# Local attention, channel mix and conv GLU on one core: mix in six chunks across batches, pooled queries and keys summed on VectorE or GpSimd, another order of steps

## The chip, the core and the metric

One core of a Trainium2 chip runs the whole program in one launch. TensorE (PE) does the matrix products into PSUM, VectorE (DVE) and ScalarE (ACT) work elementwise, GpSimd (POOL) does small elementwise work and issues the DMAs that add while they write, SyncE (SP) issues the plain DMAs. The metric is the device time of one launch in microseconds, the median over runs. In the profile times count from the start of the span.

## The reference

Three stages follow each other. `q`, `k` and `v` are 4 batches of 8 heads, 576 positions, 64 wide; everything is float32.

```python
q_d = q.reshape(B, H, Sd, 4, D).mean(axis=3)          # k_d, v_d alike: 576 -> 144 positions
out_up = np.repeat(sm_attn(q_d, k_d, v_d), 4, axis=2)
mask = np.abs(pos[:, None] - pos[None, :]) < 4         # a band of 7 positions
scores = np.where(mask, scale * (q @ k.T), -1e9)
x = out_up + softmax(scores) @ v                       # x: 4 x 576 x 512
x_prev = x moved by one position, zeros first
xk = mu_k * x + (1 - mu_k) * x_prev                    # xr alike with mu_r
v = np.maximum(xk @ w_k, 0) ** 2 @ w_v                 # 512 -> 1024 -> 512, the mix
x1 = sigmoid(xr @ w_r) * v
h = np.maximum(x1 @ w_in, 0)                           # 512 -> 1024
out = (h * sigmoid(conv3(h, conv_w))) @ w_out          # 1024 -> 512
```

## The kernel before

The channels lie on the 128 partitions, the tokens along the free dimension; `T` = 2304 tokens in all. To keep float32 accuracy on the fast matmul path every factor is cut into a high and a low part, and a product of 128 x 128 weights is three matmuls (high x high, low x high, high x low). `weight` brings one 512 KB tile of raw bits through `st_d` (a ring of three), rebuilds the float on ScalarE and VectorE into `st_f` or `st_ff`, and writes high and low parts (`wk`, `wv`, `wr`, `wi`, `wo`).

*Attention.* `group(b, gp)` is four heads of one batch: there are two groups a batch, eight in all. A group loads queries and keys (`kq`), overlapping windows of values (`vw`) and pooled values (`vd`), computes banded scores (L564) and pooled scores (L629), exponentials and their normalisation, transposes (L705, L756), the pooled output (L724) and the local output (L775), and adds the two into `xT`, a ring of two batches. For batch 0 the pooled keys and queries `kqd` are summed by VectorE (L527). For batches 1 to 3 the host hands in four planes `kqp`; `load_sum` loads the first plane by SyncE and adds the other three by GpSimd's DMAs, each of which waits for the one before it. `vd` is brought in the same way. From batch 1 on there is one buffer each for `kq`, `kqd`, `vw` and `vd`.

*Mix.* `mix_prep(b, nh)` makes the mixed input of half a batch, 288 tokens, in four 128-channel tiles: ScalarE scales `x_prev`, VectorE adds the scaled `x`, ScalarE writes the high part and VectorE the low part into `xk` (two buffers). The first half batch, `first_mix`, runs on plain float32 weights while these arrive. The other seven are `mix(b, nh)`: eight up groups of 12 matmuls (L933), each followed by relu, square and the cut into `k2`, and eight down groups of 12 (L982), whose results go to DRAM as `v_d`. Two PSUM buffers `mm` alternate.

*Output half.* Six chunks of 384 tokens: `gate` (L1254), `hidden` (L1295) with the convolution on VectorE, `outp` (L1375). Its tiles lie where the mix's tiles lay: the gate's input in `xk`, `x1` in `k2`, two buffers `v` for the mix's results. `w_r` and half of `w_in` (`wi0`) are cut early into the pool `mid`, which opens when the tiles of the pool `first` (batch 0's second buffers, `st_ff`) are free; the other half (`wi1`) and `v` lie in a pool that opens when the attention is done.

*Order.* Each piece of work is a `step` with an engine and the keys that it reads and writes. The list `ORDER` says in which order the steps are emitted, so also how each engine's queue stands, and `SECOND` which of two possible engines a step takes. Engines work their queues in order; between engines semaphores wait.

## Time and profile before

| | |
|---|---|
| runs (3) | 575.22, 577.9, 578.13 us; median 577.9 |
| profiled execution | 576.07 us, span 574.4 us |
| granted TensorE clock, mean | 0.986 |
| TensorE busy | 551.3 us, 96% |
| VectorE, ScalarE busy | 393.7 us, 306.0 us |
| moved by DMA | 73.34 MB |

Busy shares are means over stages that differ: in the first stretch weights arrive and the attention of batch 0 runs, then mix and attention share the engines, and from about 319 us on the output half runs. What ends a wait is named by the engine and line that released it. A matmul's own time in the profile is longer than its step to the next, since matmuls overlap; lengths of runs of matmuls are read from the chain of waits.

### The profile page before, as it was taken

The page shows a single profiled execution, that of the slowest core. Times are in us where ns is not written, and L with a number is a line of the kernel's source. Part 1 is how long each engine was busy: PE and PEld are TensorE (multiplying, and loading weights), DVE is VectorE, ACT ScalarE, POOL GpSimd, SP SyncE. Part 2 cuts the span into 40 slices and gives each one's busy share as a digit, 9 for nine tenths or more (in the row PEclk, how much of TensorE's full clock was granted, in tenths as well). Part 3 has the DMA queues.
Part 4 walks back from the last instruction along what each step waited for, and adds up shares of the span by engine and source line. Part 5 has one row for each costly group of instructions (what it writes and reads, how often), then busy time and mean ns, then how long its engine had stood idle before and what let it go on. Part 6 is the DMA issues. An engine that isn't in the chain of part 4 may idle for free.

```text
span 574.4 us, 13973 instructions
## 1 busy us (share of the span) xinstructions
PE 551.3 (96%) x5796; PEld 504.5 (88%) x5796; DVE 393.7 (69%) x807; ACT 306.0 (53%) x738; POOL 45.7 (8%) x150
## 2 busy tenths in 40 slices
PE   6898999959999999899999999999999999999996
PEld 3676689959999999899999999999998998998985
DVE  5897777727557745566747678887876677655680
ACT  4777776636455565435548557465445454353341
POOL 5011012112111111000000000000000000000000
PEclk9989999979999999999999999999999999999999
DMA  8578795969686776317323230122100401010011
GB/s 338 183 172 239 244 308 124 316 131 342 158 201 169 173 233 153 95 38 266 114 79 126 92 138 9 48 93 74 56 2 18 148 1 46 11 55 2 0 38 73
DMA packets 31008, 73.34 MB, mean 128 GB/s; under 512 B 3168, under 2 KB 13920, under 8 KB 29920
## 3 DMA queue, kind: packets, MB, share of 16 engines
q1 hardware_dynamic: 26624, 64.18, 32.2%
q0 software_dynamic: 4320, 8.26, 9.1%
q8 instruction: 45, 0.74, 0.5%
q14 instruction: 19, 0.16, 0.1%
HBM read 58.28 MB, written 14.16 MB: 126 GB/s over the span
## 4 chain that ended last, share of the span: by engine, by line
PE 81%; DMA 9%; ACT 4%; DVE 3%; issue 2%; SPq 0%; POOL 0%; ACTq 0%; POOLq 0%; DVEq 0%
PE a L1375 17%; PE mm L933 15%; PE mm L982 12%; PE a L1295 8%; PE mm L1295 7%; PE a L1254 4%; PE mm L1254 4%; DMA st_d<-in_moe_w_v 3%; DMA kqd<-in_kqp 3%; PE a L775 2%; PE a L564 2%; PE mm L900 1%; PE a L724 1%; DMA v_d<-tmp 1%; DMA vw<-in_vw 1%
## 5 line engine op out<-in xcount | busy, mean ns | idle before, releaser
L1375 PE MATMUL a<-wk,wv 128*128 128x512 f32 x432 | 101.2, 390 | 0.0
L933 PE MATMUL mm<-xk,wk 128*128 128x288 f32 x672 | 94.6, 298 | 1.8 <-ACT tmp L917 1.5
L982 PE MATMUL mm<-k,wv 128*128 128x288 f32 x672 | 95.4, 298 | 0.1
L1375 PEld LDWEIGHTS a<-wk,wv 128*128 128x128 f32 x432 | 80.9, 188 | 15.6
L933 PEld LDWEIGHTS mm<-xk,wk 128*128 128x128 f32 x672 | 90.2, 189 | 3.1 <-ACT tmp L917 1.8
L982 PEld LDWEIGHTS mm<-k,wv 128*128 128x128 f32 x672 | 90.0, 188 | 1.6 <-issue 1.0
L1295 PE MATMUL mm<-k,wi 128*128 128x386 f32 x288 | 54.0, 338 | 0.3 <-DVE k L1281 0.3
L1295 PE MATMUL a<-k,wi 128*128 128x386 f32 x288 | 53.6, 338 | 0.4 <-ACT h L1323 0.4
L1295 PEld LDWEIGHTS mm<-k,wi 128*128 128x128 f32 x288 | 50.8, 188 | 1.3 <-DVE k L1281 0.8
L1295 PEld LDWEIGHTS a<-k,wi 128*128 128x128 f32 x288 | 50.8, 188 | 1.3 <-ACT h L1323 0.7
L1350 ACT ACTIVATE tmp<-tmp 128x384 f32<-128x384 f32 x48 | 24.7, 524 | 45.0 <-DVE tmp L1344 45.0
L952 ACT ACTIVATE tmp<-mm 128x288 f32<-128x288 f32 x56 | 22.8, 411 | 33.1 <-PE mm L933 24.2
L1362 DVE TENSOR_TENSOR wv<-tmp,wv 128x384 fp32r<-128x384 f32 x48 | 26.2, 553 | 12.8 <-ACT wv L1360 12.6
L1353 DVE SCALAR_TENSOR_TENSOR tmp<-tmp,h 128x384 f32<-128x384 f32 x48 | 26.4, 556 | 12.1 <-ACT tmp L1350 10.7
L1360 ACT CAST wv<-tmp 128x384 fp32r<-128x384 f32 x48 | 24.2, 510 | 14.9 <-DVE tmp L1353 14.9
L1344 DVE SCALAR_TENSOR_TENSOR tmp<-h,cw_sb,tmp 128x384 f32<-128x384 f32 x48 | 29.7, 619 | 2.6
L1341 DVE SCALAR_TENSOR_TENSOR tmp<-h,cw_sb,tmp 128x384 f32<-128x384 f32 x48 | 29.7, 618 | 2.6 <-DVE tmp L1340 0.5
L970 DVE TENSOR_TENSOR k<-tmp,k 128x288 fp32r<-128x288 f32 x56 | 24.9, 456 | 8.5 <-ACT k L963 6.6
L917 ACT COPY tmp<-mm 128x288 f32<-128x288 f32 x32 | 12.3, 399 | 27.6 <-PE mm L982 18.1
L1340 DVE TENSOR_SCALAR tmp<-h,cw_sb 128x384 f32<-128x384 f32 x48 | 20.0, 417 | 9.7 <-ACT h L1323 4.4
L1254 PE MATMUL a<-xk,wr 128*128 128x386 f32 x144 | 26.2, 337 | 0.0
L1254 PE MATMUL mm<-xk,wr 128*128 128x386 f32 x144 | 26.1, 337 | 0.0
(160 smaller groups left out, 848.6 us busy)
## 6 DMA issues: line engine op xcount, KB each, us to landing
vw<-in_vw SPq DMA_DIRECT2D x7, 1152.0 KB, 8.9
kq<-in_kq SPq DMA_DIRECT2D x6, 1152.0 KB, 10.2
...
```

Source lines behind the costliest of these rows:

```text
L933: nc.tensor.matmul(pst[:, 0:NH], lhsT=wk_t[wt][:, kt, mt * P:(mt + 1) * P], rhs=xk[:, xs, kt, :], start=(kt == 0 and g == 0), stop=(kt == ...
L970: ("DVE",), (dve(NH),), lambda e, r=r, kh=kh, kl=kl: e.tensor_sub(kl, r, kh.bitcast(F32)),
L982: nc.tensor.matmul(pst[:, 0:NH], lhsT=wv_t[wt][:, kt, mt * P:(mt + 1) * P], rhs=xs, start=(kt == 0 and g == 0), stop=(kt == KF - 1 and g = ...
L1254: nc.tensor.matmul(pst[:, 0:CW], lhsT=late["wr"][wt][:, kt, mt * P:(mt + 1) * P], rhs=r_t[xs][:, kt, :], start=(kt == 0 and g == 0), stop= ...
L1295: nc.tensor.matmul(pst[:, 0:CW], lhsT=late["wi%d" % (mt * P // HF)][wt][:, kt, mt * P % HF:mt * P % HF + P], rhs=x1s[xs][:, kt, :], start= ...
L1341: nc.vector.scalar_tensor_tensor(out=cv, in0=tap(0), scalar=cw[:, 0, mt:mt + 1], in1=cv, op0=ALU.mult, op1=ALU.add)
L1344: nc.vector.scalar_tensor_tensor(out=cv, in0=tap(2), scalar=cw[:, 2, mt:mt + 1], in1=cv, op0=ALU.mult, op1=ALU.add)
L1350: step("ACT", act(CH), lambda: nc.scalar.activation(cv, cv, AF.Tanh, scale=0.5), (), [cvk])
L1353: lambda: nc.vector.scalar_tensor_tensor(out=gt, in0=cv, scalar=1.0, in1=tap(1), op0=ALU.add, op1=ALU.mult),
L1360: step("ACT", act(CH), lambda: nc.scalar.copy(gh, gf), ["wv_old", gk], [("gh", j)])
L1362: ("DVE",), (0.56,), lambda e: e.tensor_sub(gl, gf, gh.bitcast(F32)),
L1375: nc.tensor.matmul(pst, lhsT=xs[:, tt * P:(tt + 1) * P], rhs=wo[wt][:, kt, :], start=(kt == 0 and g == 0), stop=(kt == KF - 1 and g == 2),)
```

## The change

Six chunks of tokens replace the eight half batches: two of 288 and four of 432, which run across batch borders, so a chunk's input is put together from one or two batches' `xT`. `xk`, `k2` and `tmp` are 432 wide; there is one `xk` instead of two, and `xk` and `k2` lie in the pool `mid`, where `wi0` lay. All of `w_in` goes to the late pool. One of the two `v` buffers lies in `mid`, the other in the dead part of `k2`. `kqp` is gone: from batch 1 on each group's pooled keys and queries are summed from `kq`, by one reduction on VectorE or three additions on GpSimd, as `SECOND` says; nine of the twelve halves go to GpSimd. `ORDER` and `SECOND` are new lists; the warm-up matmuls stand at the front.

```diff
...
     NH = S // 2
+    NT = 3 * S // 4
+    chunks_ = [(0, NH), (NH, NH)] + [(t, NT) for t in range(S, B * S, NT)]
+    K2 = 9
...
-    xk_t = several(main, 2, [P, 2, KM, NH], F32R, "xk")
-    K2 = 9
-    k2_t = several(main, 2, [P, K2, NH], F32R, "k2")
-    tmp = main.tile([P, 8, NH], F32, name="tmp")
+    tmp = main.tile([P, 8, NT], F32, name="tmp")
...
-            if b:
-                d, dk = g["kqd"]
-                load_sum(
-                    d.rearrange("p r s -> p (r s)"), [kqp[b, gp, :, t] for t in range(FAC)], 4 * SD,
-                    [(dk, i, pr) for i in (0, half) for pr in range(2)], SL[0],
-                )
...
+                def f(eng, t=t, d=d):
+                    o = d[:, a // FAC:e // FAC]
+                    i = t[:, a:e].rearrange("p (s t) -> p s t", t=FAC)
+                    if eng is nc.vector:
+                        eng.reduce_sum(o, i, axis=AX.X)
+                    else:
+                        eng.tensor_tensor(out=o, in0=i[:, :, 0], in1=i[:, :, 1], op=ALU.add)
+                        for j in range(2, FAC):
+                            eng.tensor_tensor(out=o, in0=o, in1=i[:, :, j], op=ALU.add)
...
+                ws = [(dk, i0, pr)] + ([(dk, half, pr)] if whole else [])
+                if b:
+                    step(
+                        both, (0.15 + 1.05e-3 * (e - a), 3 * pool((e - a) // FAC)), f, [(k, i0)], ws,
+                        slack=SL[i0 > 0],
                     )
...
+    def mix_prep(i):
+        t0, n = chunks_[i]
+        prog.tag = "mp", i
+        parts = []
+        for b in range(t0 // S, (t0 + n - 1) // S + 1):
+            parts.append((b, max(t0 - b * S, 0), min(t0 + n - b * S, S)))
...
+            xs = [("xT", b % 2, kt, c) for b, a, e in parts for c in (0, half) if (c == 0 or e > NH)]
+
+            def scaled(t=t, kt=kt):
+                for b, a, e in parts:
+                    o = b * S + a - t0
+                    nc.scalar.activation(
+                        t[:, o:o + e - a], xT[b % 2][:, kt, a:e], AF.Copy, scale=mus[:, 2, kt:kt + 1])
+
...
+            def whole(t=t, f=f, kt=kt):
+                for b, a, e in parts:
+                    o = b * S + a - t0
+                    nc.vector.scalar_tensor_tensor(
+                        out=f[:, o:o + e - a], in0=xT[b % 2][:, kt, 1 + a:1 + e], scalar=mus[:, 0, kt:kt + 1],
+                        in1=t[:, o:o + e - a], op0=ALU.mult, op1=ALU.add)
+
...
+            step(
+                "ACT", act(n), lambda kt=kt, f=f: nc.scalar.copy(late["xk"][:, 0, kt, 0:n], f), [fk, "mid"],
+                [("xk", 0, kt)],
+            )
...
-                            pst[:, 0:NH], lhsT=wk_t[wt][:, kt, mt * P:(mt + 1) * P], rhs=xk[:, xs, kt, :],
+                            pst[:, 0:n], lhsT=wk_t[wt][:, kt, mt * P:(mt + 1) * P], rhs=late["xk"][:, xs, kt, 0:n],
...
     def open_mid():
         first.release()
         late["mid"] = mid = tc.alloc_tile_pool(name="mid", bufs=1, reuse_waits="tile")
+        late["xk"] = mid.tile([P, 2, KM, NT], F32R, name="xk")
+        late["k2"] = several(mid, 2, [P, K2, NT], F32R, "k2")
         late["wr"] = several(mid, 2, [P, KM, DM], F32R, "wr")
-        late["wi0"] = several(mid, 2, [P, KM, HF], F32R, "wi0")
-
-    seconds = [("kq", 2), ("kq", 3), ("st_f", 2), ("st_f", 3)] + [(x, 1) for x in ("kqd", "vw", "vd", "probs", "pd")]
+        late["v"] = several(mid, 1, [P, KM, CW], F32, "v")
+
+    seconds = [("st_f", 2), ("st_f", 3)] + [(x, 1) for x in ("kq", "kqd", "vw", "vd", "probs", "pd")]
     step("", 0.0, open_mid, (), [k for k in prog.writer if root(k, seconds)] + ["mid"])
     late["two"] = True
     by_columns(w_r, lambda: late["wr"][0], lambda: late["wr"][1], KM, range(KM), "wr", ["mid"])
-    by_columns(
-        w_in, lambda: late["wi0"][0], lambda: late["wi0"][1], KM, range(KF // 2), "wi", ["mid"],
-    )
-    mixes = [(b, nh) for b in range(B) for nh in range(2)]
-    for i, (b, nh) in enumerate(mixes):
-        xk_next = None
-        if nh == 0:
-            store_x(b)
-        if i:
-            mix(b, nh, *xk)
-        if nh == 0 and b + 1 < B:
-            gs = [group(b + 1, gp) for gp in range(NG)]
-            for g in gs:
-                g["loads"](0, NB)
-                attend([g], 0, NB)
-        if i + 1 < len(mixes):
-            xk = mix_prep(*mixes[i + 1])
+    store_x(0)
+
+    def attend_batch(b):
+        for g in [group(b, gp) for gp in range(NG)]:
+            g["loads"](0, NB)
+            attend([g], 0, NB)
+
+    attend_batch(1)
+    mix_prep(1)
+    for i in range(1, len(chunks_)):
+        mix(i)
+        if i == 1:
+            store_x(1)
+        elif i < B:
+            attend_batch(i)
+            store_x(i)
+        if i + 1 < len(chunks_):
+            mix_prep(i + 1)
...
-        late["wi1"] = several(wb, 2, [P, KM, HF], F32R, "wi1")
-        late["v"] = several(wb, 2, [P, KM, CW], F32, "v")
+        late["wi"] = several(wb, 2, [P, KM, DFF], F32R, "wi")
...
+    def v_t(i):
+        if i:
+            return cutout(late["k2"][0], KM * CW, KM * CW, F32).rearrange("p (k c) -> p k c", k=KM)
+        return late["v"][0]
...
```

Three places of the new order. The first is TensorE's queue around the pooled scores of batch 2, group 0 (`kqd` read, `mm` the mix's PSUM), before:

```order
L775 MATMUL a_181<-pt_139,vw_133 64x32 x36
L775 MATMUL a_182<-pt_139,vw_133 64x32 x36
L982 MATMUL mm_178<-k_123,wv_117 128x288
...
L629 MATMUL a_182<-kqd_131 32x144 x20
...
L564 MATMUL a_181<-kq_129 32x38 x40
L933 MATMUL mm_177<-xk_122,wk_115 128x288
```

and now:

```order
L769 MATMUL a_177<-pt_135,vw_129 64x32 x36
L769 MATMUL a_178<-pt_135,vw_129 64x32 x36
L935 MATMUL mm_174<-xk,wk_115 128x288
...
L623 MATMUL a_178<-kqd_127 32x144 x20
...
L558 MATMUL a_177<-kq_125 32x38 x72
L985 MATMUL mm_173<-k_1205,wv_117 128x288
```

Before, batch 1's last local outputs were followed by three down groups, then came the pooled scores; now they stand behind the last up group of mix chunk 1, one group after those outputs, and the down groups come after them.

The second is VectorE's queue from the last weight tile of the first chunk (`st_ff`) to the inputs of mix chunk 1 (`xk`), before:

```order
L394 SCALAR_TENSOR_TENSOR st_ff_150<-st_d_110,st_ff_150 128x512
L854 TENSOR_TENSOR xk_121<-tmp,xk_121 128x288
L844 SCALAR_TENSOR_TENSOR tmp<-xT_119,mus,tmp 128x288 x2
L854 TENSOR_TENSOR xk_121<-tmp,xk_121 128x288 x2
L580 TENSOR_REDUCE sums_145<-a_181 128x2x9
```

and now:

```order
L383 SCALAR_TENSOR_TENSOR st_ff_146<-st_d_110,st_ff_146 128x512
L421 CAST wv_117<-st_ff_146 128x4x128
L840 SCALAR_TENSOR_TENSOR tmp<-xT_119,mus,tmp 128x288
L512 TENSOR_REDUCE kqd_127<-kq_125 128x288
L421 CAST wv_117<-st_ff_145 128x4x128
L425 TENSOR_TENSOR wv_118<-st_f_113,wv_117 128x4x128
...
L425 TENSOR_TENSOR wv_118<-st_ff_145,wv_117 128x4x128
L784 TENSOR_TENSOR xT_120<-a_177,od_139 128x9x32 x2
L784 TENSOR_TENSOR xT_120<-a_178,od_139 128x9x32 x2
L854 TENSOR_TENSOR xk<-tmp,xk 128x288 x2
L840 SCALAR_TENSOR_TENSOR tmp<-xT_119,mus,tmp 128x288 x2
L854 TENSOR_TENSOR xk<-tmp,xk 128x288 x2
```

The weight cuts, one pooled sum and the attention output of batch 1, group 0 now stand between the last weight tile and the first write of `xk`.

The third is GpSimd's queue for batches 2 and 3, before (it begins in batch 2):

```order
L386 DMA kqd_131<-in_kqp 128x576 x2
L386 DMA vd_135<-in_vp 80x512 x3
L386 DMA kqd_131<-in_kqp 128x576 x3
```

and now (the last of the four `vd` DMAs and the two behind it are those of batch 3, group 0, whose pooled sums are the additions that follow):

```order
L375 DMA vd_131<-in_vp 80x512 x4
L1211 MEMSET v_1209 128x4
L375 DMA vd_131<-in_vp 80x512 x2
L514 TENSOR_TENSOR kqd_127<-kq_125 128x288
L516 TENSOR_TENSOR kqd_127<-kqd_127,kq_125 128x288 x2
```

The adding DMAs of the pooled keys are gone from the queue, and the additions stand behind the adding DMAs of the values.

## Rows read from the trace of the kernel before

**Rows 1.** The page: busy time, share of the span and instructions of each engine.

```profile
PE 551.3 (96%) x5796; PEld 504.5 (88%) x5796; DVE 393.7 (69%) x807; ACT 306.0 (53%) x738; POOL 45.7 (8%) x150
```

**Rows 2.** Windows: stretch and length, busy per engine (instructions), clock, DMA share, GB/s.

```profile
5.60:74.60 69.00, 63.37 (x1124) 45.66 (x1123) 59.45 (x135) 48.30 (x124) 9.85 (x30) 0.95 0.73 230
45.50:74.60 29.10, 26.33 (x446) 19.28 (x445) 22.63 (x48) 22.16 (x56) 4.32 (x5) 1.00 0.75 225
78.20:574.40 496.20, 482.72 (x4652) 455.05 (x4651) 331.48 (x667) 253.13 (x605) 31.39 (x102) 0.99 0.37 111
120.00:130.00 10.00, 5.77 (x153) 4.65 (x160) 1.60 (x4) 3.24 (x14) 1.72 (x3) 0.66 0.65 127
```

**Rows 3.** Timeline of PE behind its longest wait: start, length, instructions [idle before].

```profile
124.23 1.69 PE L629 MATMUL a<-kqd 64*32 64x144 f32 x40 [5.80 <-DMA kqd<-in_kqp]
...
126.53 1.15 PE L564 MATMUL a<-kq 64*32 64x38 f32 x80
127.61 2.36 PE L933 MATMUL mm<-xk,wk 128*128 128x288 f32 x12
```

**Rows 4.** Timeline of POOL: DMAs that add, two stretches.

```profile
111.59 0.86 POOL L386 DMA_DIRECT2D kqd<-in_kqp  x1 [7.07 <-DMA kqd<-in_kqp]
119.43 0.87 POOL L386 DMA_DIRECT2D kqd<-in_kqp  x1 [6.98 <-DMA kqd<-in_kqp]
...
188.82 0.81 POOL L386 DMA_DIRECT2D vd<-in_vp  x1 [3.02 <-DMA vd<-in_vp]
192.62 0.81 POOL L386 DMA_DIRECT2D vd<-in_vp  x1 [2.98 <-DMA vd<-in_vp]
```

**Rows 5.** Chain that ended last: start, length, what; full runs of matmuls.

```profile
267.71 12.69 PE mm L933 x96
...
293.18 12.85 PE mm L933 x96
...
384.26 2.72 PE a L1375 x12
```

**Rows 6.** Timeline of PE: the same forms without a wait before.

```profile
64.09 0.96 PE L629 MATMUL a<-kqd 64*32 64x144 f32 x40
...
70.16 0.91 PE L564 MATMUL a<-kq 64*32 64x38 f32 x80
...
80.42 1.83 PE L933 MATMUL mm<-xk,wk 128*128 128x288 f32 x12
```

**Rows 7.** Groups by form on DVE: count | busy us, mean ns | idle before.

```profile
L790 DVE TENSOR_TENSOR xT<-a,od 128x288 f32<-128x288 f32 x24 | 9.7, 451 | 14.6 <-PE a L775 9.6 <-issue 4.9
...
L527 DVE TENSOR_REDUCE kqd<-kq 128x224 f32<-128x896 f32 x2 | 2.1, 1080 | 4.7 <-DMA kq<-in_kq 4.7
...
L432 DVE CAST wi<-st_f 128x512 fp32r<-128x512 f32 x4 | 1.7, 420 | 0.0
```

**Rows 8.** Groups by form on POOL.

```profile
L345 POOL MEMSET probs<- 128x1152 f32 x1 | 1.1, 1057 | 0.0
```

**Rows 9.** DMA issues: count, KB each, median us to landing.

```profile
kq<-in_kq SPq DMA_DIRECT2D x6, 1152.0 KB, 10.2
...
vd<-in_vp SPq DMA_DIRECT2D x6, 160.0 KB, 3.6
```

**Rows 10.** Chain that ended last: a weight wait, and the start of the mix.

```profile
58.61 6.99 DMA st_d<-in_moe_w_v
...
78.20 1.59 PE mm L933 x12
...
98.65 4.32 DMA kqd<-in_kqp
```

**Rows 11.** Timeline of DVE: last weight tile of the first chunk, a pass of 684 columns.

```profile
73.88 0.69 DVE L394 SCALAR_TENSOR_TENSOR st_ff<-st_d,st_ff 128x512 uint32<-128x512 uint32 x1
...
77.50 0.87 DVE L580 TENSOR_REDUCE sums<-a 128x18 f32<-128x684 f32 x1
```

**Rows 12.** Windows, line L933 alone: up matmuls between 78.2 and 98.65 us.

```profile
78.20:98.65 20.45, 13.82 (x96) 12.65 (x95) 1.00 0.74 219
```

More of the change, by code (lines that the diff above doesn't have):

```diff
@@ L859, in first_mix @@
+                lambda kt=kt, f=f: nc.vector.tensor_sub(
+                    late["xk"][:, 1, kt, 0:n], f, late["xk"][:, 0, kt, 0:n].bitcast(F32)),
+                [fk, ("xk", 0, kt), "mid"], [("xk", 1, kt)],
+            )
+        return fs
     def first_mix(xs):
@@ L910, in first_mix, with out_of_mix, mix @@
                 weight(w_v, lambda: wv_t[0], lambda: wv_t[1], a, 4, mt * P, "wv", use=down)
-            prog.tag = "dn", 0, 0
+            prog.tag = "dn", 0
             out_of_mix(mt, pst, pk, 0)
-    def out_of_mix(mt, pst, pk, t0):
-        i = count["vs"] = count.get("vs", -1) + 1
-        vs, vk = tmp[:, 6 + i % 2], ("tmp", 6 + i % 2)
-        step("ACT", act(NH), lambda: nc.scalar.copy(vs, pst[:, 0:NH]), (), [pk, vk])
+    def out_of_mix(mt, pst, pk, i):
+        t0, n = chunks_[i]
+        j = count["vs"] = count.get("vs", -1) + 1
+        vs, vk = tmp[:, 6 + j % 2, 0:n], ("tmp", 6 + j % 2)
+        step("ACT", act(n), lambda: nc.scalar.copy(vs, pst[:, 0:n]), (), [pk, vk])
         step(
-            "SP", dma_us(NH), lambda: nc.sync.dma_start(out=v_d[mt, :, t0:t0 + NH], in_=vs),
+            "SP", dma_us(n), lambda: nc.sync.dma_start(out=v_d[mt, :, t0:t0 + n], in_=vs),
             [vk], [("v_d", t0, mt)],
         )
-    def mix(b, nh, xk, key):
-        c0 = nh * NH
-        k2 = {}
-        prog.tag = "up", b, nh
+    def mix(i):
+        t0, n = chunks_[i]
+        prog.tag = "up", i
+        at = {}
         for mt in range(KF):
@@ L959, in square, with high @@
                     e.tensor_tensor(out=r, in0=r, in1=r, op=ALU.mult)
-            def high(e, r=r, kh=kh):
+            def high(e, r=r, j=j):
+                kh = late["k2"][0][:, j, 0:n]
                 if e is nc.scalar:
@@ L1107, in tile_local_attention__then__channel_mix__then__conv_glu @@
     by_columns(
-        w_in, lambda: late["wi1"][0], lambda: late["wi1"][1], KM, range(KF // 2, KF), "wi", ["late"], HF,
+        w_in, lambda: late["wi"][0], lambda: late["wi"][1], KM, range(KF), "wi", ["late"],
     )
@@ L1157, in tile_local_attention__then__channel_mix__then__conv_glu @@
     step("", 0.0, lambda: None, (), [k for k in prog.writer if k[0] == "xT" and k[1] == 1] + ["xT1"])
-    for i in range(2):
-        step("", 0.0, lambda: None, (), [k for k in prog.writer if k[0] == ("xk", i)] + [("xk_old", i)])
+    step("", 0.0, lambda: None, (), keys_of("xk") + ["xk_old"])
     step("", 0.0, lambda: None, (), keys_of("k2") + ["k2_old"])
@@ L1194, in vpads @@
         def vpads():
-            v = late["v"][vi]
+            v = v_t(vi)
             if lo == 0:
@@ L1201, in load_chunk @@
         if lo == 0 or hi == T:
-            step("POOL", 0.15, vpads, ["late"], [("v", vi)])
-        t0s = [t for t in range(0, T, NH) if t < e and t + NH > a]
+            step("POOL", 0.15, vpads, [v_old[vi]], [("v", vi)])
+        t0s = [t for t, n in chunks_ if t < e and t + n > a]
         step(
@@ L1206, in load_chunk @@
             lambda: nc.sync.dma_start(
-                out=late["v"][vi][:, :, a - lo + 1:e - lo + 1], in_=v_d[:, :, a:e].rearrange("k p s -> p k s")),
-            ["late"] + [("v_d", t, mt) for t in t0s for mt in range(KM)], [("v", vi)],
+                out=v_t(vi)[:, :, a - lo + 1:e - lo + 1], in_=v_d[:, :, a:e].rearrange("k p s -> p k s")),
+            [v_old[vi]] + [("v_d", t, mt) for t in t0s for mt in range(KM)], [("v", vi)],
         )
```

134 lines of the change are left out of this document (54 added, 80 removed), and 184 rows, old and new, of tables (ORDER, SECOND).

## The prediction

> **What bounds the kernel now.** I read the page's busy shares first: TensorE is busy 551.3 of 574.4 us [rows 1], so the reader should look for what TensorE's time is made of and for the few places where it waits. The windows by stage come next. They show two regimes [rows 2]. Up to about 74.6 us VectorE leads (59.45 of 69.0 us busy, and 59.45 - 22.63 = 36.8 of the 39.9 us before 45.5); there TensorE is "busy" with long, thin work. From 78.2 us to the end TensorE is busy 482.7 of 496.2 us at a mean clock of 0.99: every matmul taken out there shortens the run, and so does every wait. The waits of TensorE in time order then name one large wait: at 118.4 us it stands 5.80 us before the pooled scores of batch 2 (L629), released by the DMA that adds up the pooled keys and queries [rows 3]. The POOL timeline says why that is late: each of the three adding DMAs waits for the one before it, and they follow each other at 7.84 us (111.59 to 119.43) there, against 3.80 us at 188.82 to 192.62 [rows 4].
>
> The sum is made against the profiled execution: span 574.4 us, 576.07 us as timed, so 1.7 us lie around the span. It is 0.3% below the median of the runs, 577.9 us. Half a per cent (575.0 to 580.8 us) is about what a measurement of this kernel can tell from no change.
>
> **Fewer matmuls in the mix.** Seven mix chunks of 288 tokens with 192 matmuls each (the first chunk is worked otherwise and stays) become one of 288 and four of 432: 1344 matmuls become 960. Columns stay the same, since 1152 x 288 = 768 x 432. A matmul of 288 columns takes 12.69 / 96 = 132.2 ns in a full run of them, one of 512 takes 2.72 / 12 = 226.7 [rows 5]; on the line between them 432 columns come to 192.9 ns. So 1152 x 132.2 - 768 x 192.9 = 152.3 - 148.2 = 4.1 us; by the slowest full run of 96 (12.85) it is 154.2 - 148.6 = 5.6. I take 4.1. This lies in the stretch where TensorE ends last, so all of it counts.
>
> *A rule against this size.* The rows have some 12 ns per matmul beside its columns (132.2 - 288/2.4). The Trainium skill (TensorE: Matmul & The Clock Gate, Back-to-back issue gap) gives 2.5 ns for a warm one; by it the 384 matmuls less would be worth 1.0 us. The rows disagree with it here, and the measurement decides.
>
> **The adding DMAs go.** All 24 transfers of the pooled queries and keys go, 18 of them adding ones. The wait of 5.80 us goes with them. Behind it TensorE ran slower for a while: 40 pooled scores took 1.69 us against 0.96, 80 scores 1.15 against 0.91, 12 mix matmuls 2.36 against 1.83 [rows 3, 6], 1.5 us together; the granted clock of that stretch was 0.66 [rows 2], part of it at 1.2 instead of 2.4 GHz, after the idle time. So 7.3 us go. What is late there next is the sum that replaces them, below.
>
> **The sums on GpSimd and VectorE.** Twelve pooled halves: nine go to GpSimd as three additions each of 288 columns, three to VectorE as one reduction. VectorE: 1.08 us for 896 columns [rows 7], so 1.39 for 1152. GpSimd shows no two-input addition. The nearest row is a memset of 1152 columns, 1.06 us [rows 8]; a quarter of it, 0.26, is the lower bound, all of it the upper. An addition moves three streams of 288 columns, 864, so I take 0.8 us: 2.4 us for a half, 4.8 for both. Now three walks to the place where TensorE needs them:
> - Batch 2, group 0 (the old wait): the queries and keys land 10.2 us after issue [rows 9], then 4.8 us of sums, 15.0. TensorE has in between seven groups of 12 at 1.59 and attention pieces of 5.7 (from their lengths between 78.2 and 98.65): 16.8 us. No wait.
> - Batch 2, group 1: VectorE does one half and stands for the load; behind it in its queue are the normalisation and the last half of the next chunk's inputs. 10.2 + 0.4 of issue, 1.4, two passes of 0.87 and a small one (2.0), three 432-wide steps (0.6 each, between 0.45 and 0.69) and a ScalarE copy of 0.5: 16.3 us. TensorE has eight groups at 1.59 and 2.9 us of attention: 15.6. It waits 0.7 us.
> - Batch 3, group 0: both halves stand on GpSimd's queue behind three adding DMAs for the values. Landing of the first load 3.6 us [rows 9], two spacings of 3.8, 0.8 for issuing the third, 4.8 of sums: 16.8 us. TensorE has five groups of 2.33 and some 5.3 of attention: 16.9. Just in time.
>
> I book 1.0 us, with the hops between engines. What is queued behind a late sum on GpSimd are only the next values' DMAs.
>
> **The order at the start of the mix.** Before, mix chunk 1 starts at 78.2 us, 3.6 us after VectorE finished the last weight tile of the first chunk (73.88 + 0.69) [rows 10, 11]. Now its input tile lies where the first tiles lay, so it can be written only after the last of these is free, and the attention of batch 1, group 0 is put ahead of it. VectorE's order says how much it must do. Up to the last weight tile: four passes over 684 columns (0.87 each), three casts (0.42) and small ones of 0.6 more, six 288-wide steps (0.45 each) less: 3.5 + 1.3 + 0.6 - 2.7 = 2.7 us more [rows 7, 11]. VectorE idles 29.1 - 22.6 = 6.5 us in the second half of that stretch, for weights on their way. With less traffic a part may go, anything from none to all; I take 0.8, near the low end, since nothing else of the loads' order is lighter. So the last tile is done at 74.6 + 2.7 - 0.8 = 76.5. After it: two casts 0.84, the reduction 1.39, three 512-wide steps of 0.69 2.1, twelve 288-wide ones 5.4, a ScalarE copy 0.4: 10.1. Mix chunk 1 starts at 86.7, 8.5 us later. But by then TensorE has done what it did before between 78.2 and 98.65 beside its 96 mix matmuls: 20.45 - 12.7 = 7.7 us [rows 5, 10, 12]. Net 0.8 us lost. In those 10.1 us TensorE has only 5.4 us to do, so it idles about as long as in [rows 3]; I book the same 1.5 us of lower clock. Bounds: with all idle gone 4.9 us gained; with one more weight wait like the one of 6.99 us [rows 10], 8 us lost.
>
> **What costs nothing.** One input tile instead of two: its next writing waits for the last up matmul, and a down half of 8 x 1.59 or 8 x 2.33 us lies over it (the ScalarE copy that waits has the next exponentials behind it, the 1.0 us above holds them). All of w_in loaded after the attention: two chunks of 192 x 0.194 = 37 us hide eight tiles; uncovered, a tile would cost its landing, about 5 us. The output half keeps its matmuls. The warm-up matmuls put in front lie before the first scores, where VectorE leads.
>
> **Sum:** -4.1 - 7.3 + 1.0 + 0.8 + 1.5 = -8.1: span 566.3, 568.0 us as timed.
>
> **Rivals.**
> 1. *The start gets shorter.* VectorE's 6.5 us of idle for weights vanish with the traffic. For it: the DMA queues stand at 0.75 there [rows 2]. Against: the weights' loads still queue behind the large loads on SyncE. 568.0 - 5.7 = 562.3 us.
> 2. *GpSimd's additions hold VectorE up.* Nine of the 27 additions fall before mix chunk 1, where VectorE leads: if VectorE stands still in them, 9 x 0.8 = 7.2 us go on the path: 575.2 us, no change. The rows of before have no such pair side by side. (The Trainium skill, GPSIMD Engine Reference, Key points, says the two share SBUF interfaces when VectorE reads two inputs from SBUF; no run here shows it yet.)
> 3. *The wait comes back on GpSimd's queue, slower than before.* Batch 3, group 0: if the value DMAs follow at the 7.84 us of [rows 4] and not at 3.8, the chain is 3 x 7.84 + 5.6 = 29.1 us against 16.9: TensorE stands 12.2 us and then runs 1.5 us of lower clock: 568.0 + 13.7 = 581.7. It decides from a spacing of 6.6 us on, where 3s + 5.6 - 16.9 + 1.5 eats the 9.9 us against the median; from 7.5 us on it is slower by over half a per cent. For it: that is what happened to batch 2. Against: those spacings fell with 288 KB adding transfers, which are gone.
>
> **How the numbers follow.** Forecast 0.56, rival 1 0.19, rival 2 0.13, rival 3 0.12. The forecast's own range is 563 to 574 (the bounds of the start, 0.26 to 1.06 us per addition, 4.1 to 5.6 us for the matmuls). 559 to 580 leaves out rival 3 and little else. Faster than 575.0: 0.93 of the forecast, all of rival 1, a third of rival 2: 0.75. Slower than 580.8: rival 3 but for its lower edge, and a little of 2: 0.11. Same: 0.14.
>
> **What would show it.** In the profile after: no wait for pooled keys over 2 us anywhere; 96 matmuls of 432 columns in 18.5 us; the first mix matmul with the new tile near 86.7 us, after some 5 us of idle TensorE; GpSimd additions of about 0.8 us; the output half as long as before. Wrong it would be by a start after 92 us, by a TensorE wait at batch 3's pooled scores, or by additions above 1.1 us.

## The result and the profile after

The changed kernel takes 568.27 us (median of 4 runs, 566.07 to 568.48) beside 577.34 us of the kernel before (also 4 runs): ratio 0.984, 95% interval 0.9803 to 0.9877. 568.0 was predicted. The total was met, by terms of which several were off and cancel.

The page of the profiled execution (568.25 us, span 566.5), its row of busy times, answers to [rows 1]:

```profile
PE 547.7 (97%) x5412; PEld 496.8 (88%) x5412; DVE 397.6 (70%) x758; ACT 307.2 (54%) x715; POOL 57.6 (10%) x159
```

The windows by stage after the change, columns as in [rows 2] (stretch and length, busy time of TensorE, its weight loads, VectorE, ScalarE and GpSimd, clock, DMA share, GB/s): the last weight tiles of the first chunk, the way to mix chunk 1, the mix with the rest of the attention, the output half.

```profile
45.50:76.60 31.10, 29.52 (x450) 23.09 (x450) 28.62 (x54) 23.11 (x56) 3.24 (x4) 1.00 0.81 265
76.60:86.60 10.00, 7.39 (x282) 5.78 (x280) 9.91 (x18) 6.47 (x15) 5.71 (x7) 0.92 0.42 99
86.61:308.70 222.09, 221.28 (x2672) 206.91 (x2673) 143.06 (x262) 124.80 (x294) 29.12 (x38) 0.99 0.46 148
308.70:566.50 257.80, 252.29 (x1296) 233.94 (x1295) 179.92 (x341) 124.56 (x277) 5.13 (x64) 1.00 0.15 53
```

The kernel before, profiled anew (run before_again, span 574.1), the two stages that answer to the last two rows:

```profile
77.85:318.51 240.66, 233.12 (x3360) 223.49 (x3358) 153.16 (x329) 131.67 (x332) 24.98 (x40) 0.99 0.60 177
318.51:574.10 255.59, 250.24 (x1297) 232.00 (x1295) 179.13 (x340) 121.78 (x273) 5.60 (x62) 1.00 0.14 49
```

Read them as a sum: mix chunk 1 starts 8.8 us later, the mix is 18.6 us shorter, the output half 2.2 us longer, together 7.6 us. In the mix TensorE stands 222.09 - 221.28 = 0.8 us where it stood 240.66 - 233.12 = 7.5. In the second row VectorE is busy 9.91 of 10.0 us: it sets the start of the mix, and has nothing to wait for there.

The timeline of TensorE at the start of the mix, and at the place of the old wait [rows 3]:

```profile
83.53 0.96 PE L623 MATMUL a<-kqd 64*32 64x144 f32 x40 [1.73 <-DVE xT L784]
...
84.85 1.11 PE L558 MATMUL a<-kq 64*32 64x38 f32 x80
86.61 3.25 PE L935 MATMUL mm<-xk,wk 128*128 128x288 f32 x12 [0.65 <-ACT tmp L919]
...
90.65 3.92 PE L935 MATMUL mm<-xk,wk 128*128 128x288 f32 x24
...
109.12 0.96 PE L623 MATMUL a<-kqd 64*32 64x144 f32 x40
```

The first matmul with the new tile comes at 86.61 us. The last row shows the pooled scores of batch 2, group 0: no wait, 0.96 us for 40 as in [rows 6]. But behind the waits of 1.73 and 0.65 us the matmuls at the start run at the lower clock, 1.2 GHz (granted 0.50 from 86 to 90 us, 0.56 from 90 to 92): 12 in 3.25 us.

The chain that ended last, full runs of matmuls (as [rows 5]):

```profile
233.62 18.73 PE mm L935 x96
...
369.36 2.13 PE mm L1309 x12
```

96 matmuls of 432 columns take 18.73 us (18.79 the slowest), 195.1 ns each.

The timeline of GpSimd for batch 3, group 0 (as [rows 4]): the second and third of the adding DMAs for the values, then the pooled sums; behind it TensorE's pooled scores.

```profile
159.31 0.80 POOL L375 DMA_DIRECT2D vd<-in_vp  x1 [2.77 <-DMA vd<-in_vp]
162.95 0.80 POOL L375 DMA_DIRECT2D vd<-in_vp  x1 [2.84 <-DMA vd<-in_vp]
163.50 1.00 POOL L514 TENSOR_TENSOR kqd<-kq 128x288 f32<-128x288 f32 x1
...
167.99 2.29 POOL L516 TENSOR_TENSOR kqd<-kqd,kq 128x288 f32<-128x288 f32 x2
```

```profile
170.34 0.93 PE L623 MATMUL a<-kqd 64*32 64x144 f32 x32 [0.29 <-POOL kqd L516]
```

The DMAs follow at 3.6 to 3.7 us, the two sums take 6.8 us and end at 170.3; TensorE's pooled scores wait 0.29 us for them, the longest wait for pooled sums in the mix.

The timeline of VectorE beside GpSimd's additions, then the same two instructions in the run sums_vector (below), where GpSimd adds nothing:

```profile
77.39 1.35 DVE L512 TENSOR_REDUCE kqd<-kq 128x288 f32<-128x1152 f32 x1
...
78.98 1.43 DVE L425 TENSOR_TENSOR wv<-st_f,wv 128x512 fp32r<-128x512 f32 x1
80.34 1.20 DVE L840 SCALAR_TENSOR_TENSOR tmp<-xT,mus,tmp 128x288 f32<-128x288 f32 x1
```

```profile
79.91 0.68 DVE L422 TENSOR_TENSOR wv<-st_f,wv 128x512 fp32r<-128x512 f32 x1
80.51 0.51 DVE L837 SCALAR_TENSOR_TENSOR tmp<-xT,mus,tmp 128x288 f32<-128x288 f32 x1
```

GpSimd adds from 77.58 to 81.2 us. The two instructions with two inputs in SBUF inside that time take 1.43 and 1.20 us; without the additions they take 0.68 and 0.51. The reduction, with one input, keeps its 1.35.

### The profile page after: what moved, and what is told of

It reads as the page before. It is cut to its first block, busy times and chain, and to the rows that moved or that the text cites. A ratio compares the mean times of both kernels' runs of the same rounds, so it can differ in the third digit from the quotient of the medians.

```text
span 566.5 us, 13091 instructions
## 1 busy us (share of the span) xinstructions
PE 547.7 (97%) x5412; PEld 496.8 (88%) x5412; DVE 397.6 (70%) x758; ACT 307.2 (54%) x715; POOL 57.6 (10%) x159
## 3 DMA queue, kind: packets, MB, share of 16 engines
q0 software_dynamic: 1728, 2.95, 3.2%
## 4 chain that ended last, share of the span: by engine, by line
PE 78%; DVE 12%; DMA 3%; ACT 3%; issue 2%; POOL 1%; ACTq 0%; DVEq 0%; POOLq 0%; SPq 0%
PE a L1389 17%; PE mm L935 15%; PE mm L985 14%; PE mm L1309 8%; PE a L1309 8%; PE a L1268 5%; PE mm L1268 4%; DMA st_d<-in_moe_w_v 2%; PE a L769 2%; PE a L558 1%; PE a L750 1%; PE a L718 1%; PE a L699 1%; DVE st_f L380 1%; DVE st_f L383 1%
## 5 line engine op out<-in xcount | busy, mean ns | idle before, releaser
L935 PE MATMUL mm<-xk,wk 128*128 128x432 f32 (+1 forms) x480 | 94.5, 353 | 0.7 <-ACT tmp L919 0.7
L985 PE MATMUL mm<-k,wv 128*128 128x432 f32 (+1 forms) x480 | 91.1, 347 | 0.0
L935 PEld LDWEIGHTS mm<-xk,wk 128*128 128x128 f32 x480 | 86.0, 193 | 4.5 <-ACT tmp L919 1.0
L985 PEld LDWEIGHTS mm<-k,wv 128*128 128x128 f32 x480 | 84.2, 188 | 3.6 <-issue 0.4
L954 ACT ACTIVATE tmp<-mm 128x432 f32<-128x432 f32 (+1 forms) x40 | 20.2, 508 | 25.4 <-PE mm L935 20.8
L380 DVE SCALAR_TENSOR_TENSOR st_f<-st_f,st_d 128x512 uint32<-128x512 uint32 x28 | 21.1, 752 | 18.2 <-ACT st_d L399 18.2
L974 DVE TENSOR_TENSOR k<-tmp,k 128x432 fp32r<-128x432 f32 (+1 forms) x40 | 22.8, 579 | 12.3 <-ACT k L966 11.6
```

The costliest lines, as they stand in the source:

```text
L380: nc.vector.scalar_tensor_tensor(out=f, in0=f, scalar=3, in1=low, op0=ALU.logical_shift_left, op1=ALU.bitwise_or)
L935: nc.tensor.matmul(pst[:, 0:n], lhsT=wk_t[wt][:, kt, mt * P:(mt + 1) * P], rhs=late["xk"][:, xs, kt, 0:n], start=(kt == 0 and g == 0), sto ...
L985: nc.tensor.matmul(pst[:, 0:n], lhsT=wv_t[wt][:, kt, mt * P:(mt + 1) * P], rhs=late["k2"][xs][:, at[kt], 0:n], start=(kt == 0 and g == 0), ...
```

## The experiments

**Both kernels again.** No edit. The question is a difference that the change doesn't explain: 12 matmuls of 386 columns in the output half follow in 2.13 us, before in 2.10.

> The kernel before, unchanged, for a profile on the chip of the runs beside it. In the profiled runs so far 12 matmuls of 386 columns follow in 2.10 us before the change and in 2.13 after it, which is 1.3 us over the 48 x 12 of L1295 / L1309 alone, and nothing of them was changed. Theory: the length belongs to the chip or the execution; then before and after agree here to 0.01 us per 12. Rival: it belongs to the program (where tiles lie, what runs beside); then 2.10 and 2.13 come again, and the output half is again 255.7 us before and 257.8 after.

> The changed kernel, unchanged. Time 566 to 569 us, ratio 0.980 to 0.988. Theory (chip or execution): full runs of 96 matmuls of 432 columns as long as twelve times eight would be on the line through this chip's own 288 and 512 columns, and the output half as long as that of the kernel before on this chip to 0.5 us. Rival (program): 18.75 us for 96 and an output half 2.1 us longer than before.

Measured: 575.83 us for the profiled run of before (one run), 569.08 after, ratio 0.9867 (0.9841 to 0.9893) to 17 runs of before on that chip. There before has 2.10 to 2.11 again, after 2.13, and 18.73 us for 96 of 432 columns. The length belongs to the program, not to the chip.

**All pooled sums on VectorE.**

```diff
-    3, 7, 22, ..., 266, 278, 279, 290, 314, 325, ..., 472, 496, 497, 508, 532, ..., 618, 642, 643, 677, 689, ...
+    3, 7, 22, ..., 266, 290, 325, ..., 472, 508, ..., 618, 689, ...
```

> The changed kernel with all pooled sums on VectorE, none on GpSimd. Theory: GpSimd's additions stretch VectorE's two-input instructions that run beside them (0.68 to 1.43 us, 0.51 to 1.20 us; 4.3 us of excess before mix chunk 1), so VectorE is no worse off with three reductions of 1.35 us more (4.05 us): first mix matmul with the new tile at 86.6 +- 1.0 us, time within 1.5 us of the changed kernel. Rival: the additions cost VectorE nothing on its path; then the first such matmul comes 4 us later, at 90.6, and the time is 571 to 573 us.

Measured: 569.3 us, ratio 0.9876 (0.9848 to 0.9903), the same as the changed kernel beside it. Start of the mix:

```profile
86.10 3.25 PE L932 MATMUL mm<-xk,wk 128*128 128x288 f32 x12 [0.69 <-ACT tmp L916]
```

86.10 us, and not 90.6, with 4.05 us more of reductions on VectorE ahead of it. GpSimd takes no load off VectorE here: what it takes over ahead of the mix, VectorE loses to longer instructions.

**One part of the change in the kernel before.** For the last five groups additions on GpSimd stand where two of the three adding DMAs were issued.

```diff
-                load_sum(
-                    d.rearrange("p r s -> p (r s)"), [kqp[b, gp, :, t] for t in range(FAC)], 4 * SD,
...
+                    def add(prs, t=t, d=d):
+                        for pr in prs:
+                            o = d[:, pr, 0:2 * SD]
+                            i = t[:, pr, 0:2 * S].rearrange("p (s t) -> p s t", t=FAC)
+                            nc.gpsimd.tensor_tensor(out=o, in0=i[:, :, 0], in1=i[:, :, 1], op=ALU.add)
+                            for j in range(2, FAC):
+                                nc.gpsimd.tensor_tensor(out=o, in0=o, in1=i[:, :, j], op=ALU.add)
...
+                step("SP", 0.0, lambda: None, (), ks)
+                step("GQ", 0.0, lambda: None, (), ks)
+                step("GQ", 2.4, lambda: add(() if late_ else (0,)), () if late_ else [(k, 0)], ks)
+                step("GQ", 2.4, lambda: add((0, 1) if late_ else (1,)), [(k, 0)], ks)
```

> The kernel before with one part of the change alone: for the last five groups the adding DMAs of the pooled queries and keys are replaced by additions on GpSimd at the places in its queue where the last two adding DMAs of each group were issued; chunks, tiles and the rest of the order stay. Theory: the 5.8 us wait and the 1.5 us of slower clock behind it are the adding DMAs' price, so 7.3 us go: 570 us, ratio 0.987, no wait of TensorE for pooled keys over 1 us. Rival: the wait is only handed on, to the additions or to the value DMAs behind them: 575 us or more, ratio above 0.995.

Measured: 574.77 us, ratio 0.9974 (0.9951 to 0.9997). The theory fails on the time: of 7.3 us some 1.5 were gained. VectorE's timeline, while GpSimd adds from 83.9 to 91.0 us, then TensorE's:

```profile
85.04 1.18 DVE L436 TENSOR_TENSOR wv<-st_ff,wv 128x512 fp32r<-128x512 f32 x1 [0.96 <-ACT wv L430]
86.15 1.44 DVE L391 SCALAR_TENSOR_TENSOR st_f<-st_f,st_d 128x512 uint32<-128x512 uint32 x1
87.62 1.47 DVE L394 SCALAR_TENSOR_TENSOR st_f<-st_d,st_f 128x512 uint32<-128x512 uint32 x1
89.01 1.23 DVE L976 TENSOR_TENSOR tmp<-tmp 128x288 f32<-128x288 f32 x1
90.16 1.20 DVE L987 TENSOR_TENSOR k<-tmp,k 128x288 fp32r<-128x288 f32 x1
```

```profile
94.00 6.13 PE L950 MATMUL mm<-xk,wk 128*128 128x288 f32 x24 [1.42 <-ACT tmp L969]
...
116.95 6.56 PE L999 MATMUL mm<-k,wv 128*128 128x288 f32 x36
123.44 0.96 PE L646 MATMUL a<-kqd 64*32 64x144 f32 x40
...
143.00 1.86 PE L999 MATMUL mm<-k,wv 128*128 128x288 f32 x12 [1.71 <-ACT tmp L969]
```

Five instructions that take 0.69, 0.68, 0.69, 0.46 and 0.46 us in before_again take 3.5 us more in all. VectorE is late with the mix's `k`, ScalarE with the relu that empties the PSUM buffer, TensorE waits 1.42 us and then needs 6.13 us for 24 matmuls (3.44 in before_again), at a granted clock of 0.50. At 116.95 another 36 take 6.56 us instead of 5.03, again at 0.50, though TensorE had stood no longer than 0.24 us just before; why the clock fell there is open. So it comes to the pooled scores at 123.44, when the sums are ready, and only 0.9 us before the 124.37 of before_again. With the full clock behind it TensorE is 3.0 us ahead at 127.4 (before_again 130.35), and loses that again beside the next group's additions (136.8 to 143.2): it waits 0.68, 1.71 and 0.83 us where before_again waits 0.35, and at the pooled scores of group 1 it is 0.2 us behind (160.29 against 160.11). The lost time was not gone; it had moved beside the additions.

**The same with one input on GpSimd.** The kernel leaves out the sums: each of the three passes scales one position of four.

```diff
-                            nc.gpsimd.tensor_tensor(out=o, in0=i[:, :, 0], in1=i[:, :, 1], op=ALU.add)
-                            for j in range(2, FAC):
-                                nc.gpsimd.tensor_tensor(out=o, in0=o, in1=i[:, :, j], op=ALU.add)
+                            for j in range(1, FAC):
+                                nc.gpsimd.tensor_scalar(o, i[:, :, j], float(FAC), 0.0, op0=ALU.mult, op1=ALU.add)
```

> As before_sums, but GpSimd's three passes of each half read one input instead of two (scale of one position of four; the sum itself is left out). Theory: what ate the 7.3 us in before_sums are VectorE's two-input instructions that ran beside GpSimd's two-input additions (0.46 to 1.23 us, 0.69 to 1.47 us between 85.0 and 91.3 us) and held TensorE up behind them; with one input they keep their 0.46 and 0.69 us, TensorE has no wait over 1 us there, and the time is 569 to 571.5 us. Rival: VectorE is stretched beside any GpSimd pass, or the gain was lost elsewhere: 574 to 576 us.

Measured: 571.43 us, ratio 0.9929 (0.9903 to 0.9955), between before_sums and the changed kernel. VectorE and TensorE at the same places:

```profile
86.61 1.18 DVE L391 SCALAR_TENSOR_TENSOR st_f<-st_f,st_d 128x512 uint32<-128x512 uint32 x1
87.83 0.70 DVE L394 SCALAR_TENSOR_TENSOR st_f<-st_d,st_f 128x512 uint32<-128x512 uint32 x1
88.44 0.97 DVE L975 TENSOR_TENSOR tmp<-tmp 128x288 f32<-128x288 f32 x1
89.38 0.91 DVE L986 TENSOR_TENSOR k<-tmp,k 128x288 fp32r<-128x288 f32 x1
```

```profile
93.49 3.44 PE L949 MATMUL mm<-xk,wk 128*128 128x288 f32 x24 [0.26 <-ACT tmp L968]
...
119.20 0.96 PE L645 MATMUL a<-kqd 64*32 64x144 f32 x40
```

With one input VectorE is stretched less (1.18 instead of 1.44, 0.97 instead of 1.23; the 0.70 instead of 1.47 falls mostly between GpSimd's two halves, 87.3 to 88.2 us), the wait ahead shrinks to 0.26 us, the full clock stays, and TensorE is at the pooled scores 4.2 us sooner. The theory holds in its direction and falls in its detail: GpSimd's passes hold VectorE up with one input too, only less. The Trainium skill (SBUF — State Buffer, SBUF: two separate sides) says that VectorE and GpSimd share one pair of ports, that an instruction holds it to its end, and that VectorE wants it where it has two inputs in SBUF, against a GpSimd instruction that reads SBUF. The rows agree: about twice the length for those, none more for the reduction.

**The adding DMAs put back into the changed kernel.**

```diff
+                    def plane(eng, d=g["kqd"][0]):
+                        nc.sync.dma_start(out=d.rearrange("p r s -> p (r s)"), in_=kqp[b, gp, :, 0])
...
+                    def adds(eng, d=g["kqd"][0]):
+                        for j in range(1, FAC):
+                            nc.gpsimd.dma_start(
+                                out=d.rearrange("p r s -> p (r s)"), in_=kqp[b, gp, :, j], accum_op=ALU.add)
...
-                        both, (0.15 + 1.05e-3 * (e - a), 3 * pool((e - a) // FAC)), f, [(k, i0)], ws,
-                        slack=SL[i0 > 0],
+                        both, (0.15, 0.15), adds if pr else plane, [],
+                        [(dk, x, y) for x in (i0, half) for y in range(2)], slack=SL[i0 > 0],
```

> The changed kernel with the four planes of pooled queries and keys and their adding DMAs put back for all six groups (plane 0 on SyncE right behind the pooled scores that read the tile last, the three adding DMAs on GpSimd next to that place); chunks, tiles and the rest of the order are those of the changed kernel. Theory of the prediction: the adding DMAs are worth 7.3 us against 1.0 for the sums, so the time is 573 to 576 us, with a wait of TensorE for pooled keys of some 4 to 6 us at batch 2. Rival: in the new order the pooled scores of batch 2 come late enough and VectorE is freed of the additions' stretch; no wait over 1 us, the time within 1.5 us of the changed kernel or below it, and the gain then belongs to the order, not to the sums.

Measured: 578.93 us, ratio 1.0028 (0.9998 to 1.0058); the profiled run is the fastest of 12 (574.66). Its TensorE and GpSimd:

```profile
86.76 1.58 PE L632 MATMUL a<-kqd 64*32 64x144 f32 x40 [2.83 <-DMA kqd<-in_kqp]
...
114.39 1.69 PE L632 MATMUL a<-kqd 64*32 64x144 f32 x40 [2.64 <-DMA kqd<-in_kqp]
```

```profile
93.73 1.10 POOL L526 DMA_DIRECT2D kqd<-in_kqp  x1
104.21 0.86 POOL L526 DMA_DIRECT2D kqd<-in_kqp  x1 [9.38 <-DMA kqd<-in_kqp]
```

The whole gain of the change is gone. The adding DMAs follow at 10.5 us here, TensorE waits for them twice and runs at the lower clock after each (granted 0.50 from 88 to 90, 0.57 from 114 to 116). It also waits 1.62 us for pooled values at 100.43, whose DMAs share GpSimd's queue. The profiled execution shows 6.5 us of the loss (span 573.0 against 566.5); where the median loses the rest no trace shows. So with these DMAs in these places the new chunks and order are worth nothing, and the sums without the order 1.5 us (before_sums): the gain needed both. Other places might cost less, and were not tried.

**Two matmuls of 216 columns for one of 432.**

```diff
+def cols(n, later):
+    return [(0, n)] if n < 432 or not later else [(0, n // 2), (n // 2, n)]
...
-                        nc.tensor.matmul(pst[:, 0:n], ..., rhs=late["xk"][:, xs, kt, 0:n], ...)
+                        for c0, c1 in cols(n, kt or g):
+                            nc.tensor.matmul(pst[:, c0:c1], ..., rhs=late["xk"][:, xs, kt, c0:c1], ...)
```

> The changed kernel with each mix matmul of 432 columns cut into two of 216, but for the first of each PSUM tile: 720 matmuls more, the same columns. Theory: what a matmul takes beside its columns (132.2 - 120 = 12.2 ns at 288, 195.6 - 180 = 15.6 at 432) is a price for each one, near 12 ns at 216, so a pair is 2 x 102.2 = 204.4 instead of 195.6: 720 x 8.8 = 6.3 us more, about 575 us. Rival 1: 2.5 ns for each, the rest hangs on the columns: 1.8 us more, 570.5. Rival 2: at 216 columns the loading of weights no longer fits behind the matmul, and a pair is longer by far: over 580.

Measured: 593.67 us, ratio 1.0314. A full run of the chain, and the longest of TensorE's waits (us in total, times, longest):

```profile
247.22 21.23 PE mm L940 x184
```

```profile
PE a L562 <- issue: 5.0, 2, 2.7
```

88 splits cost 21.23 - 18.73 = 2.50 us, 28.4 ns each: a matmul of 216 columns takes (195.1 + 28.4) / 2 = 111.8 ns, 21.8 beside its columns. 720 x 28.4 ns are 20.4 us, and 5.0 more go in two waits that the profile puts down to issue, that is, for which it shows no releaser. The time is rival 2's: there is no fixed price for each matmul (12.2 ns at 288 columns, 15.1 at 432, 13.4 at 512, 21.8 at 216), so a straight line through two widths is no forecast for a third. That the loading of weights is what holds a narrow matmul up, as rival 2 has it, is not shown. The Trainium skill (TensorE: Matmul & The Clock Gate, LDWEIGHTS (loading the stationary operand)) gives columns / 1.2 ns for a load, so some 107 ns for 128 columns, as an estimate. The 111.8 ns lie just above it, but the trace's own records of these loads last 188 to 193 ns each and overlap, so they don't settle it.

**The tiles of the output half at their old addresses modulo 128.**

```diff
-        late["k2"] = several(mid, 2, [P, K2, NT], F32R, "k2")
+        late["k2"] = several(mid, 1, [P, K2, NT], F32R, "k2a")
+        late["gap"] = [mid.tile([P, 16], F32, name="gap0")]
+        late["k2"] += several(mid, 1, [P, K2, NT], F32R, "k2b")
+        late["gap"] += [mid.tile([P, 16], F32, name="gap1")]
...
+        late["gap"] += [wb.tile([P, 16], F32, name="gap2")]
...
-        return cutout(late["xk"], x * KM * CW, KM * CW, F32R)...
+        return cutout(late["xk"], x * (KM * CW + 8), KM * CW, F32R)...
```

> The changed kernel with three unused gaps of 64 bytes and one offset of 32: the tiles of the output half (k2 low, wr, wi, the gate's low input) begin at the same address modulo 128 as before the change. Theory: its 386-column matmuls are longer after the change (12 in 2.13 us, before 2.10) because of where their tiles lie; then 12 take 2.10 to 2.11 us and the output half 255.7 us instead of 257.8: 2 us less time, while 432-column matmuls stay at 195.6 ns. Rival: not the address modulo 128, but something else in the program; then 2.13 and 257.8 stay, and so does the time.

Measured: 565.74 us, ratio 0.9828 (0.9782 to 0.9874). Chain and output half:

```profile
232.91 18.74 PE mm L935 x96
...
368.29 2.10 PE mm L1313 x12
```

```profile
307.84:564.30 256.46, 250.64 (x1296) 231.94 (x1295) 179.90 (x341) 124.46 (x277) 5.14 (x64) 1.00 0.16 53
```

12 matmuls of L1313 take 2.10 us again, the output half 1.3 us less of the 2.2 it had lost, and the 432-column matmuls stay as they were. So the length of a 386-column matmul hangs on where its tiles lie; which of the four shifts did it was not taken apart, and the other 0.9 us of the output half is open. That the total fell is likely, not shown: the interval overlaps those of the changed kernel.

**The mix's input first.** VectorE writes all of `xk` before the attention output of batch 1, group 0 and the pooled sum of group 1; TensorE does two up groups ahead of the scores.

```diff
-    313, 195, 314, ..., 306, ..., 304, 321, ..., 315, ..., 312, 357, 185, 322, 358, 183, 323, 316, 359, 363,
+    195, ..., 312, 314, 357, 306, 304, 313, 185, 358, 183, 359, 363, 321, 315, 322, 323, 316,
```

> The changed kernel with another order at the start of the mix: VectorE writes all of mix chunk 1's input before it takes up the attention output of batch 1, group 0 and the pooled sum of group 1; GpSimd's half of that sum stands behind the value DMAs; TensorE does two up groups of chunk 1 before the pooled and local scores of group 1. Theory: VectorE is the bound there (9.9 of 10.0 us busy), 1.54 + 1.35 us of its work and about 1.5 us of stretch by the additions go behind the start: first mix matmul at 82.2 us instead of 86.6, TensorE hardly idle, no slower clock behind it (2.4 us now): 3 to 5 us less time. Rival: the attention of group 1 comes later by as much, and TensorE waits for it before the mix's down half: time within 1 us of the changed kernel.

Measured: 571.13 us, ratio 0.992 (0.9894 to 0.9945): slower than the changed kernel.

```profile
83.81 4.86 PE L935 MATMUL mm<-xk,wk 128*128 128x288 f32 x24 [3.38 <-ACT tmp L919]
...
110.74 0.96 PE L623 MATMUL a<-kqd 64*32 64x144 f32 x40
```

The mix starts 2.8 us sooner, after a wait of 3.38 us and still at the lower clock, and the next batch's pooled scores come 1.6 us later (110.74 against 109.12). In this order a sooner start of the mix is worth nothing. TensorE afterwards waits 0.67 us for exponentials and 1.26 for the pooled output of batch 1, which suggests that this attention decides there; the next two experiments test that.

**The gap filled with idle matmuls,** on top of aligned.

```diff
+WARM = {321: 13, 358: 5}
...
         for i in self.order():
+            for _ in range(WARM.get(i, 0)):
+                self.warm()
```

> The kernel aligned with 18 idle matmuls of 304 columns (13 before the pooled scores of batch 1, group 1, 5 before the first matmul of mix chunk 1), where TensorE stood 2.4 us and ran at 1.2 GHz from 84.5 to 91.8 us afterwards. Theory: with the gap filled the granted clock stays at 1.00 there, 12 matmuls of chunk 1 take 1.59 instead of 3.25 and 2.28 us, and about 2.4 us go: 563.5 us. Rival: VectorE's chain of batch 1's attention sets the pace there; TensorE runs faster, then waits longer for the probabilities, and the time is that of aligned, 565.7, to 1 us.

Measured: 566.49 us, ratio 0.9812 (0.9775 to 0.985): as aligned.

```profile
87.07 1.86 PE L938 MATMUL mm<-xk,wk 128*128 128x288 f32 x12
...
100.88 0.66 PE L753 MATMUL a<-ident,probs 128*128 128x128 f32 x4 [1.05 <-ACT od L735]
```

The same first 12 matmuls in aligned:

```profile
87.49 2.95 PE L935 MATMUL mm<-xk,wk 128*128 128x288 f32 x12
```

The clock stays at 1.00, these 12 take 1.86 us and not 2.95 (3.25 in the changed kernel), and TensorE waits the longer for the probabilities (0.41 us at 99.18) and the pooled output (1.05), neither of which it does there in aligned. It comes to batch 2's pooled scores at 108.79, in aligned at 108.51. The rival holds: the lower clock was hidden under the attention's chain on VectorE and ScalarE.

**That chain shortened,** on top of aligned_warm; beside it aligned once more.

```diff
-    325, 308, 415, 368, 364, 318, ..., 362, ..., 365, 366, 367, ..., 496, 319, 330, 374, 320, 378, ..., 371, 331,
+    325, 318, 319, 320, 308, 415, 368, 364, ..., 362, ..., 365, 366, 367, ..., 496, 330, 374, 331, 378, ..., 371,
```

> The kernel aligned_warm with three steps of batch 1, group 1's attention put ahead: the sum and normalisation of its probabilities on VectorE before the k2 work of the first two up groups of chunk 1, its exponential on ScalarE before one relu, and ScalarE's copy of its pooled output before a cast that waits 2.98 us for VectorE. Theory: in aligned_warm TensorE got 2.4 us of clock back and gave them away in waits for the probabilities and the pooled output (1.4 and 1.5 us), because the attention chain of that group sets the pace at the start of the mix; with the chain shorter by about 2 us these waits fall under 0.5 us each and the time falls by 1.5 to 2.5 us: 564 us. Rival: the k2 work that is pushed back holds up the down half of chunk 1 or the two PSUM buffers instead: waits of TensorE for ScalarE's relu appear, and the time stays within 1 us of 566.

> The kernel aligned once more, beside probs_first on one chip: ratio 0.980 to 0.985 to the kernel before. It tells whether the idle matmuls and the new order together are worth more than the alignment alone: theory 1.5 us or more between the two, rival less than 1.

Measured on one chip: 565.42 us, ratio 0.9764 (0.9734 to 0.9794), and 567.13, ratio 0.9787 (0.975 to 0.9825). TensorE in probs_first:

```profile
87.23 1.86 PE L938 MATMUL mm<-xk,wk 128*128 128x288 f32 x12
...
107.04 0.96 PE L626 MATMUL a<-kqd 64*32 64x144 f32 x40
...
125.20 1.31 PE L721 MATMUL a<-pdt,vd 80*64 80x160 f32 x16 [0.68 <-ACT pdt L708]
```

From the first mix matmul to batch 2's pooled scores it is 19.8 us, where aligned_again has 22.6 and the changed kernel 22.5. To the output half 1.8 of these 2.8 us are given back, part of it in later waits like the 0.68. 1.7 us are left between the two medians, as the theory had it, but the intervals overlap: that much is likely, not shown. Against the changed kernel (0.984 and 0.9867) probs_first is faster in both comparisons, the intervals apart: it beats both kernels.

## Why the prediction was right, and where its terms were not

That the total came out at 568.27 beside 568.0 is in part luck: TensorE's waits shrank by 1.9 us more than was booked, and the output half grew by 2.2 us that nobody forecast. All terms against before_again and the profiled run after; the start is the remainder, not read off one row.

| term | predicted | measured |
|---|---|---|
| fewer matmuls in the mix | -4.1 | -2.4 by the full runs (1152 x 132.2 ns - 768 x 195.1) |
| TensorE's waits in the mix (-5.8, +1.0) | -4.8 | -6.7 (7.5 to 0.8) |
| lower clock (old 1.5 gone, 1.5 new) | 0 | +0.1 (2.1 gone, 2.2 new) |
| start of the mix against attention done by then | +0.8 | -0.8 |
| output half | 0 | +2.2 |
| sum | -8.1 | -7.6 |

The first and the fourth row can be split another way. All matmuls into `mm` in the mix, before_again and after (columns as above, without GpSimd's):

```profile
77.85:318.51 240.66, 189.23 (x1346) 180.34 (x1346) 0.00 (x0) 33.69 (x84) 0.99 0.60 177
86.61:308.70 222.09, 184.94 (x961) 170.50 (x962) 0.00 (x0) 29.44 (x59) 0.99 0.46 148
```

Here TensorE is busy 4.3 us less with them, the lower clock's share included, and not 2.4. With that the first row is near the -4.1 that was predicted, and the start comes to +1 to +2, by where the lower clock's share is counted. Which split is right, no run decides.

- *Fewer matmuls.* The mechanism is right. In full runs a matmul of 432 columns takes 195.1 ns and not 192.9, so the size by them is 2.4; by the whole stage it is 4.3. split_216 shows that a line between two widths is no safe forecast. The Trainium skill's rule that was weighed (TensorE: Matmul & The Clock Gate, Back-to-back issue gap) makes 1.0 us, an estimate from 2.5 ns a matmul. The rows don't bear its size out, 12.2 and 15.1 ns beside the columns; as a forecast it was no further off than the 4.1 if the full runs count, and further off if the whole stage does.
- *The adding DMAs.* Confirmed as a cause (with them in the places that kqp_back gives them the whole gain goes), and the 5.8 us wait is gone. But the step "so 7.3 us go" leaves out what the change's order does: before_sums gets 1.5 us from the same sums in the old order, where TensorE loses nearly as much again beside the additions.
- *The walks.* Batch 2, group 0: no wait, as said. Batch 3, group 0, "just in time": 0.29 us. DMA spacing 3.7 us where 3.8 was taken; rival 3 needed 6.6. The sums themselves were mis-sized: an addition takes (7.9 + 21.0) / 27 = 1.07 us on average and not 0.8, just under the 1.1 that was named as the sign of an error. The first addition of a half takes 0.88 us on average, the two that add into it 1.17; with hardly a two-input instruction of VectorE beside them (119.44 us) they take 0.71 and 0.99. The wait of 0.7 us for batch 2, group 1 did not come.
- *The start.* 86.61 us against 86.7, and 76.58 against 76.5 for the last weight tile, by two errors that cancel. VectorE's idle time for weights fell from 6.5 to 31.10 - 28.62 = 2.5 us, where 0.8 of it was to go; and its work in that stretch grew by 28.62 - 22.63 = 6.0 us, where 2.7 was counted, a part of it stretched instructions, 0.8 of it work that it had done before 45.5 us. Whether the net was better or worse than booked hangs on the split above.
- *Rival 2* had the right mechanism and the wrong size: VectorE doesn't stand still through 7.2 us of additions, its two-input instructions take twice as long. sums_vector shows that this costs about what the additions save, so the time is the same either way.
- *Rival 1*: the idle time for weights did shrink, by 4.0 us, but VectorE's longer work used it up. That less traffic did it is not shown: the DMA queues stand at 0.81 in that stretch, and at 0.75 before.
- *Lower clock.* The rows at 86.61 and 90.65 us take 3.25 and 3.92 us, in aligned_warm 1.86 and 3.45; with the local scores beside them that is the 2.2 us. In before_again four rows from 124.37 us on (1.69, 0.75, 1.15 and 2.68 us) make the 2.1. As a term of the sum the new part was wrong in kind: aligned_warm takes it away and the time stays.
- *"The output half as long as before"* failed: it is 2.2 us longer, 1.3 of them by where its tiles lie (aligned gives them back), the rest open.
